# Two-level last product of attention and feed-forward: later first loads, one turn of the PSUM banks, S3's results by way of GpSimd, stores carried into the next product

## The chip, the cores and the metric

The kernel runs on one core of a Trainium2 chip. The metric is the device time of one execution in microseconds (us). Five engines work beside each other, each on its own queue in order: TensorE (PE; its weight loads are listed as PEld), VectorE (DVE), ScalarE (ACT), GpSimd (POOL) and SyncE (SP), which here issues nearly all DMAs. An instruction that waits holds up everything behind it on its own queue.

## The reference, cut to what matters

All arrays are float32; B = 8, H = 12, S = 448, D = 64.

```python
q_n, k_n = rmsnorm(q, g_q), rmsnorm(k, g_k)
scores = (1 / np.sqrt(D)) * np.matmul(q_n, k_n.transpose(0, 1, 3, 2))
attn = softmax(scores)                       # over the last axis
x = np.matmul(attn, v).transpose(0, 2, 1, 3).reshape(B * S, H * D)   # 3584 x 768
h = x @ w_in                                 # 768 x 2048
g = np.maximum(h, 0.0) ** 2
out = g @ w_out                              # 2048 x 768 -> 3584 x 768
```

## The kernel before, in words

The eight batches are worked on in four spans of two. In each span the attention gives x transposed (`xT`, features on partitions, two batches of 448 tokens beside each other), the first product gives g transposed (`gT`), and the second product gives the output transposed, which is turned back and stored. While the second product of a span runs, the attention of the next span is interleaved with it. The last span has no attention beside it, and it is the only one that the change touches.

Both products use Strassen's scheme in its form with seven products of blocks, named A11, S2, S1, S3, A12, A22, S4 by the weights that they use. Sums of the weights are made once at the start and written to DRAM (`w1s`, `w2s`); sums of the right-hand side are made on the chip (`xC` and part of `xT` for the first product; `gC` and part of `gT` for the second, by `combine`, L1021, four subtractions for each f).

`first_product` (L1034) loops over f = 0 to 7. For each f it runs seven groups of three products of 128x128 by 128x448 (each is two rows in the profile). The groups add up in the PSUM tiles `pa`, `pb`, `pc`, `pd`: pa takes A11, then A12; pb S2; pc S1, then S4; pd S3, then A22. VectorE adds the intermediate sums (z, L1075; y, L1078; the results, L1083), ScalarE applies Relu (L1040), GpSimd squares (L1044). The weights of a group (`sw`, 192 KB) are loaded by SyncE through five buffers: before group k the load of group k + 4 is issued (L665, L1066). Counted over all f the groups are u = 0 to 55, N1 = 56.

`bank` (L460) deals out two PSUM banks in turn, one for each call: pb, pc, pd take three of them for each f.

`last_product` (L1144) is the second product of the last span. Its seven products come in the order A11, A12, S2, S1, S3, A22, S4 (o = 0 to 6). Each has three output blocks of 128x448, m = 0, 1, 2. Blocks 0 and 1 are made by a second level of the same scheme, with seven runs of four products of 128x128 by 128x224 (eight rows each): pa (a11), pb (s2), pc (s1), pd (s3), pa (a12), pd (a22), pc (s4). Block 2 is made plainly by `third` (L1227), with eight products by 128x448. The second level needs sums of the weights (`add_weights`, L1173: four GpSimd additions of 128x512) and of the right-hand side (`add_g`, L1185: four VectorE subtractions of 128x896); those of product o + 1 are made during product o. `load_set` (L1168) loads the 1.5 MB of weights of one product with one DMA; there are two sets, `qk` (o even) and `wb` (o odd), so `load_set(o + 2)` follows the end of product o.

A result of the outer scheme has a base, to which the product is added, and a destination. The list `into` (L1217) names them: A11 sets the tile p1s, A12 gives an output from p1s, S2 adds to p1s, S1 gives ys from p1s, S3 has two (an output from ys, and p1s added to), A22 gives an output from p1s, S4 one from ys. Where there is a base, `based` (L1252) lets GpSimd add it to the intermediate sum beforehand (za, zb from z; yb from y; 128x224 each), and `meet` (L1246) lets VectorE add the PSUM tile and write the destination. pd's second run (a22) adds to the tile that `meet(1, 1, ...)` reads, so it has to wait for that.

`send` calls `deliver` (L1137) for an output: VectorE transposes the block by 32x32 into a tile `osb` (L1139; two buffers), and four DMAs store it (L1142), on SyncE's queue unless others are named. Of the last product, S4, the third block comes last and in two halves of 224 columns, with its stores on the queues of SyncE and ScalarE.

At the end of the program (L1367 on) the last product's first two sets are loaded before the first product of the last span starts; add_weights(0) is called in its middle (u = 28), and all four add_g of product 0 after u = 54, ahead of the group S4 of f = 7. The order on each engine is the order of the program text; no planner changes it. In that order, for VectorE around the change of products: L1083 of f = 7 for A22, L1031, L1032, four add_g (L1191), L1083 for S4, then combine(7).

Of the kernel before, what the change touches and what calls it, by code (L numbers as in the profile page):

```python
# [10 lines left out]
F32 = mybir.dt.float32  # L11
# [376 lines left out]
def attention_then_ffn_bounded(  # L388
# [71 lines left out]
    def bank(name, n=None):  # L460

        turn[0] += n is None
        return ps_m.tile([P, S], F32, tag="mn"[turn[0] % 2 if n is None else n], name=name)
# [570 lines left out]
    def first_product(work, span):  # L1034
# [11 lines left out]
        for f in range(HF):  # L1046
# [6 lines left out]
            for at, i in enumerate(order):  # L1053
# [33 lines left out]
                if span and f == HF - 1 and i == S4:  # L1087
                    combine(f)
# [48 lines left out]
    def deliver(work, span, ct, col, t, queues=(nc.sync,), part=slice(0, S // 32)):  # L1137
        osb = work.tile([P, S // 32, 32], F32, tag="osb", name="osb")[:, part]
        nc.vector.transpose(osb.rearrange("p g n -> p (g n)"), ct[:, part.start * 32:part.stop * 32])  # L1139
        for i in range(0, P, 32):  # L1140
            queue = queues[i // 32 % len(queues)]
            queue.dma_start(rows[2 * span + t, :, part, col * P + i:col * P + i + 32], osb[i:i + 32])  # L1142

    def last_product(pool):  # L1144
# [13 lines left out]
        dead = [gT[:, f, 0:S] for f in range(HF)]  # L1158
        used = [0]
# [33 lines left out]
        def small_of(name):  # L1193
            return work.tile([P, HS], F32, tag=name, name=name, bufs=1)
# [4 lines left out]
        ys = dead[0:HC]  # L1199

        def place():
            used[0] += 1
            return dead[HC + used[0] % (HF - HC)]
# [5 lines left out]

        for o, i in enumerate(order):  # L1210
# [12 lines left out]
            def send(m, queues=(nc.sync,)):  # L1223
                if leaves:
                    deliver(work, NSPAN - 1, into[0][1][m], m + at[0], at[1], queues)

            def third():  # L1227
                m = HC - 1
                for part in (slice(0, HS), slice(HS, S)) if end else (slice(0, S),):
                    ps = bank("ps")[:, part]  # L1230
                    for c in range(HF):
                        nc.tensor.matmul(ps, weights_of(o, m, c // HK)[:, c % HK], rhs_of[i][:, c, part],  # L1232
                                         start=c == 0, stop=c == HF - 1)
                    for base, dst in into:
                        if base is None:
                            nc.scalar.copy(dst[m][:, part], ps)
                        else:
                            nc.vector.tensor_tensor(dst[m][:, part], base[m][:, part], ps, add)
                    if end:
                        deliver(work, NSPAN - 1, into[0][1][m], m + at[0], at[1], (nc.sync, nc.scalar),  # L1240
                                slice(part.start // 32, part.stop // 32))
                if not end:
                    add_g(o + 1, 0)
                    send(m)

            def meet(m, t, x, ps):  # L1246

                part = slice(t * HS, (t + 1) * HS)
                for (base, dst), left in zip(into, x):
                    nc.vector.tensor_tensor(dst[m][:, part], left, ps, add)  # L1250

            def based(m, t, x, name):  # L1252
                part = slice(t * HS, (t + 1) * HS)
                all = []
                for n, (base, _) in enumerate(into):
                    if base is None:
                        all.append(x)
                        continue
                    all.append(small_of(f"{name}{n}"))
                    nc.gpsimd.tensor_tensor(all[-1], x, base[m][:, part], add)  # L1260
                return all
# [5 lines left out]
            if not end:  # L1267
                third()
# [7 lines left out]
            nc.vector.tensor_tensor(y, z, pc, add)  # L1276
            add_g(o + 1, 1)
            y22 = based(1, 1, y, "yb")
            pd = ps_o.tile([P, S], F32, tag="t", name="pd")[:, 0:HS]
            run(pd, s3, t3)  # L1280
            meet(1, 1, y22, pd)
            run(pa, a12, b21, False)
            if into[0][0] is None:
                nc.scalar.copy(into[0][1][0][:, 0:HS], pa)
            else:
                meet(0, 0, [base[0][:, 0:HS] for base, _ in into], pa)
# [3 lines left out]
            send(1)  # L1290
            run(pc, s4, b22, False)
            meet(0, 1, z12, pc)
            send(0)
            add_g(o + 1, 3)
            load_set(o + 2)
            add_weights(o + 1)
            if end:
                third()
# [68 lines left out]
    with tc.tile_pool(name="last_product", bufs=2, reuse_waits="tile") as last:  # L1367
        rest = last_product(last)
        load_set, add_weights, add_g = next(rest)
        load_set(0)  # L1370
        load_set(1)
        with tc.tile_pool(name="first_product", bufs=2, reuse_waits="tile") as work:
            for u, _ in enumerate(first_product(work, NSPAN - 1)):
                if u == N1 // 2:
                    add_weights(0)
                if u == N1 - 2:
                    for n in range(4):
                        add_g(0, n)
        with tc.tile_pool(name="second_product", bufs=2, reuse_waits="tile") as work:
            rest.send(work)  # L1380
# [88 lines left out]
```

## Time and profile before

| | us |
|---|---|
| median of 3 runs | 1370.83 (1367.7 to 1371.66) |
| the profiled execution | 1369.9 |
| its span in the trace | 1368.0 |
| first product of the last span, first matmul | 1100.29 |
| last product, first matmul | 1234.17 |
| last product, last group of matmuls starts | 1355.23 |
| TensorE busy | 1337.3, 98% of the span |
| VectorE / GpSimd / ScalarE busy | 876.0 / 624.3 / 431.2 |

The mean granted TensorE clock of the span is 0.993. Times in the trace count from the span's start. In lists of groups, the busy time of a group and the mean of one instruction are followed by the idle time of its engine just before it and by what ended that idle time ("<-DVE gT L1083" is: a VectorE instruction of line 1083 that writes gT). In a table of waits, a line has the total, the number of waits and the longest. Where several rows of a timeline are merged, the row gives its number (x8); a time in brackets is the idle time before it. Each float32 matmul of the program shows as two rows of the list, so a run of four in the last product has eight.

### The profile page before, as it was taken

The numbers are of one execution on the slowest core, as the hardware profiler recorded it, in microseconds if no ns is written. First come the engines' busy times: TensorE is split into PE (matmuls) and PEld (weight loads), VectorE is DVE, ScalarE is ACT, GpSimd is POOL, SyncE is SP. The second block draws the span as 40 slices with busy tenths as digits, with TensorE's granted clock in tenths as the row PEclk, the third lists the DMA queues.
The fourth block names the chain that finished last, engine by engine and source line by source line (L and its number), as shares of the span: only waits on it lengthen the run. The fifth ranks groups of instructions, "written<-read, shape, count | busy, mean of one in ns | idle before, by whom it ended". The sixth has DMA issues, their size and how long they took to land.

```text
span 1368.0 us, 17269 instructions
## 1 busy us (share of the span) xinstructions
PE 1337.3 (98%) x5786; PEld 675.0 (49%) x5786; DVE 876.0 (64%) x1541; ACT 431.2 (32%) x680; POOL 624.3 (46%) x507
## 2 busy tenths in 40 slices
PE   8999999999999999999999999999999989998998
PEld 3333444444444555544444455444444445556877
DVE  6999788599986334478788433458787613335554
ACT  7886565433332111233333011233333101110000
POOL 4767434465573123555664122635656212322553
PEclk9999999999999999999999999999999999999999
DMA  9767998655675423346676433344764453321323
GB/s 243 228 202 203 338 350 312 186 120 118 133 141 126 102 87 86 104 111 135 130 143 130 106 87 88 100 113 109 153 130 107 104 169 87 87 75 46 113 71 86
DMA packets 413814, 190.15 MB, mean 139 GB/s; under 512 B 282388, under 2 KB 408724, under 8 KB 413716
## 3 DMA queue, kind: packets, MB, share of 16 engines
q1 hardware_dynamic: 408020, 180.44, 51.2%
q0 software_dynamic: 4736, 8.40, 2.3%
q8 instruction: 48, 0.79, 0.2%
q14 instruction: 50, 0.41, 0.1%
q10 hardware_dynamic: 960, 0.11, 0.1%
HBM read 155.72 MB, written 33.16 MB: 138 GB/s over the span
## 4 chain that ended last, share of the span: by engine, by line
PE 86%; DVE 6%; ACT 3%; DMA 2%; issue 1%; POOL 1%; SPq 0%; DVEq 0%; ACTq 0%
PE ps L1106 28%; PE pa L1068 10%; PE pd L1068 9%; PE pc L1068 9%; PE sc L785 7%; PE pav L862 7%; PE pb L1068 5%; PE ps L1232 3%; PE pd L1207 2%; ACT gT L797 1%; PE pc L1207 1%; PE pa L1207 1%; DMA sw<-w1s 1%; DVE gT L810 1%; DVE rstd L715 1%
## 5 line engine op out<-in xcount | busy, mean ns | idle before, releaser
L1044 POOL TENSOR_TENSOR gT<-gT 128x448 f32<-128x448 f32 x96 | 94.4, 985 | 294.1 <-ACT gT L1040 294.1
L1106 PE MATMUL ps<-gT,sw 128*128 128x448 f32 x576 | 225.8, 543 | 0.0
L750 POOL TENSOR_TENSOR half<-half,mhalf 128x28 f32<-128x28 f32 x36 | 174.9, 4860 | 73.4 <-DVE half L749 70.1
L1106 PE MATMUL ps<-gC,sw 128*128 128x448 f32 x432 | 170.1, 543 | 0.0
L1106 PEld LDWEIGHTS ps<-gT,sw 128*128 128x128 f32 x576 | 107.5, 190 | 113.9 <-issue 110.3
L1068 PE MATMUL pa<-xT,sw 128*128 128x448 f32 x384 | 157.2, 546 | 5.9 <-DMA sw<-w1s 5.2
L1040 ACT ACTIVATE gT<-gT 128x448 f32<-128x448 f32 x96 | 55.4, 577 | 315.7 <-DVE gT L1083 315.7
L1106 PEld LDWEIGHTS ps<-gC,sw 128*128 128x128 f32 x432 | 80.6, 190 | 86.3 <-issue 83.4
L787 ACT ACTIVATE pr<-sc 128x896 f32<-128x896 f32 x87 | 77.5, 915 | 123.0 <-PE sc L785 123.0
L1068 PEld LDWEIGHTS pa<-xT,sw 128*128 128x128 f32 x384 | 73.5, 192 | 79.1 <-issue 77.2
L785 PE MATMUL sc<-qkT 64*64 64x448 f32 (+1 forms) x1152 | 109.8, 496 | 0.0
L583 POOL TENSOR_TENSOR gC<-gC 128x384 f32<-128x384 f32 x64 | 76.3, 1211 | 62.7 <-DVE gC L579 61.0
L1083 DVE TENSOR_TENSOR gT<-z,pd 128x448 f32<-128x448 f32 x32 | 19.8, 620 | 105.4 <-PE pd L1068 105.4
L830 POOL DMA_DIRECT2D xT<-factors x72 | 38.0, 532 | 91.0 <-DMA factors<-square 53.9
L1068 PE MATMUL pd<-xT,sw 128*128 128x448 f32 x192 | 77.9, 542 | 1.4 <-DVE z L1075 1.4
L1068 PE MATMUL pd<-xC,sw 128*128 128x448 f32 x192 | 77.5, 540 | 1.3 <-DVE gT L1083 1.3
L1068 PE MATMUL pc<-xT,sw 128*128 128x448 f32 x192 | 77.5, 540 | 0.3 <-DMA sw<-w1s 0.3
L1068 PE MATMUL pb<-xC,sw 128*128 128x448 f32 x192 | 77.5, 540 | 0.2 <-DVE gT L1083 0.2
L1068 PE MATMUL pc<-xC,sw 128*128 128x448 f32 x192 | 77.4, 539 | 0.0
L752 POOL TENSOR_TENSOR qk<-qk,half 128x448 f32<-128x448 f32 x72 | 75.5, 1069 | 2.8
L862 PE MATMUL pav<-pr,vt 64*64 64x448 f32 x348 | 72.7, 537 | 0.0
L862 PE MATMUL rest<-pr,vt 64*64 64x448 f32 x348 | 72.7, 537 | 0.0
(217 smaller groups left out, 2175.4 us busy)
## 6 DMA issues: line engine op xcount, KB each, us to landing
sw<-w1s SPq DMA_DIRECT2D x224, 192.0 KB, 2.4
sw<-w2s SPq DMA_DIRECT2D x126, 256.0 KB, 3.4
w1s<-gC SPq DMA_DIRECT2D x8, 1344.0 KB, 6.4
w2s<-gC SPq DMA_DIRECT2D x8, 1344.0 KB, 6.1
out_dram<-osb SPq DMA_DIRECT2D x188, 56.0 KB, 1.8
qk<-in_q_dram SPq DMA_DIRECT2D x144, 56.0 KB, 3.5
qk<-in_k_dram SPq DMA_DIRECT2D x144, 56.0 KB, 2.9
xT<-factors POOLq DMA_DIRECT2D x72, 112.0 KB, 3.3
```

The costliest lines, as they stand in the source:

```text
L583: nc.gpsimd.tensor_tensor(*[blocks_of(n)[:, place_of(n, i)] for i in (dst, x, y)], op)
L750: nc.gpsimd.tensor_tensor(half, half, mhalf, ALU.pow)
L752: nc.gpsimd.tensor_tensor(qkn[:, s], raw[:, s], half[:, s * NG:(s + 1) * NG].rearrange("p g -> p g ()").to_broadcast([P, NG, 32]), ALU.mult)
L785: nc.tensor.matmul(sc[part, h, 0:n], qkT[rows, 0, 1, keys], qkT[rows, 0, 0, of], start=True, stop=True)
L787: nc.scalar.activation(pr, sc[:, :, 0:n], AF.Exp)
L862: nc.tensor.matmul(into, vs[i][rows, h, c, :], probs[i, c][rows, h, :], start=(c == 0), stop=(c == NF), skip_group_check=True)
L1040: nc.scalar.activation(g, src, AF.Relu)
L1044: nc.gpsimd.tensor_tensor(g, g, g, ALU.mult)
L1068: nc.tensor.matmul(ps, stream[n + at][:, c], rhs[:, c], start=first and c == 0, stop=c == HC - 1, skip_group_check=not first)
L1106: nc.tensor.matmul(ps, stream[n][:, c % 4], rhs_of[i][:, c], start=c == 0, stop=c == HF - 1)
L1207: nc.tensor.matmul(ps, lhs[:, c], rhs[:, c], start=first and c == 0, stop=c == HK - 1, skip_group_check=not first)
L1232: nc.tensor.matmul(ps, weights_of(o, m, c // HK)[:, c % HK], rhs_of[i][:, c, part], start=c == 0, stop=c == HF - 1)
```

## The change

Five things are done, all in the last span:

1. Its first loads: load_set(0) and load_set(1) are called after u = 14 and u = 21 of the first product rather than before it.
2. One turn of its banks: `turn[0] += 1` ahead of the last product, so its tiles take the other one of the two banks. Of the add_g of product 0, two stay after u = 54, two are called after u = 55, ahead of combine(7).
3. Two results of S3: VectorE writes the product's blocks 0 and 1 once, into tiles `block`, with no base (pa's half by a copy on ScalarE), and GpSimd adds each of them to its two bases (`settle`, four additions of 128x448).
4. Sums of weights: add_weights(o + 1) is called behind the run of s3 rather than at the end of product o.
5. Stores: blocks 1 and 0 of a product are not delivered at its end but in the next product, behind its third block (`late`), ahead of that product's own block 2. In S4 the third block is second in order as in all others, blocks 1 and 0 come last, and block 0 is stored in two halves. The blocks' places (`dead`) are no longer used in turn.

In the changed kernel's order on VectorE, A22 and S4 have, behind the addition of the third block (and add_g, in A22), three transposes in a row: block 1 and block 0 of the product before, then their own block 2; then zi.

```diff
-                if span and f == HF - 1 and i == S4:
+                if span and f == HF - 1 and i == S4 and span + 1 < NSPAN:
                     combine(f)
...
-        dead = [gT[:, f, 0:S] for f in range(HF)]
-        used = [0]
+        dead = [gT[:, f, 0:S] for f in range(NFC)]
+        used, late = [0], []
...
+        blocks = [work.tile([P, S], F32, tag="block", name="block") for _ in range(2)]
...
-            return dead[HC + used[0] % (HF - HC)]
+            return dead[HC - 1 + used[0]]
...
+        turn[0] += 1
         for o, i in enumerate(order):
...
-            def send(m, queues=(nc.sync,)):
-                if leaves:
-                    deliver(work, NSPAN - 1, into[0][1][m], m + at[0], at[1], queues)
+            def send(m, part=slice(0, S // 32)):
+                deliver(work, NSPAN - 1, into[0][1][m], m + at[0], at[1],
+                        (nc.sync, nc.scalar) if end else (nc.sync,), part)
+
+            both = len(into) > 1
...
-            def meet(m, t, x, ps):
+            def meet(m, t, left, ps):
 
                 part = slice(t * HS, (t + 1) * HS)
-                for (base, dst), left in zip(into, x):
-                    nc.vector.tensor_tensor(dst[m][:, part], left, ps, add)
+                dst = blocks[m] if both else into[0][1][m]
+                nc.vector.tensor_tensor(dst[:, part], left, ps, add)
 
             def based(m, t, x, name):
-                part = slice(t * HS, (t + 1) * HS)
-                all = []
-                for n, (base, _) in enumerate(into):
...
+                base = into[0][0]
+                if both or base is None:
+                    return x
+                y = small_of(name)
+                nc.gpsimd.tensor_tensor(y, x, base[m][:, t * HS:(t + 1) * HS], add)
+                return y
+
+            def settle(m):
+                for base, dst in into if both else ():
+                    nc.gpsimd.tensor_tensor(dst[m], base[m], blocks[m], add)
...
             nc.scalar.copy(p1, pa)
-            if not end:
-                third()
+            third()
+            add_g(o + 1, 0)
+            for args in late:
+                deliver(*args)
+            late[:] = []
+            if leaves:
+                send(HC - 1)
             pb = ps_o.tile([P, S], F32, tag="o", name="pb")[:, 0:HS]
             run(pb, s2, t2)
...
             run(pd, s3, t3)
+            add_weights(o + 1)
             meet(1, 1, y22, pd)
             run(pa, a12, b21, False)
...
             meet(1, 0, z21, pd)
-            send(1)
+            settle(1)
+            if end:
+                send(1)
+                send(0, slice(0, HS // 32))
             run(pc, s4, b22, False)
             meet(0, 1, z12, pc)
-            send(0)
+            settle(0)
+            if end:
+                send(0, slice(HS // 32, S // 32))
+            elif leaves:
+                for m in (1, 0):
+                    late.append((work, NSPAN - 1, into[0][1][m], m + at[0], at[1]))
             add_g(o + 1, 3)
             load_set(o + 2)
-            add_weights(o + 1)
-            if end:
-                third()
...
-        load_set(0)
-        load_set(1)
         with tc.tile_pool(name="first_product", bufs=2, reuse_waits="tile") as work:
             for u, _ in enumerate(first_product(work, NSPAN - 1)):
+                if u in (14, 21):
+                    load_set(u // 7 - 2)
                 if u == N1 // 2:
                     add_weights(0)
                 if u == N1 - 2:
-                    for n in range(4):
-                        add_g(0, n)
+                    add_g(0, 0)
+                    add_g(0, 1)
+                if u == N1 - 1:
+                    add_g(0, 2)
+                    add_g(0, 3)
+                    combine(HF - 1)
```

## The prediction

> **What bounds the kernel now.** I read the shares of busy time first, then the chain that ended last, then who waited for whom in the last 270 us (the diff touches nothing earlier), then the timeline around each wait found, and last the granted clock in short windows.
>
> ```profile
> PE 1337.3 (98%) x5786; PEld 675.0 (49%) x5786; DVE 876.0 (64%) x1541; ACT 431.2 (32%) x680; POOL 624.3 (46%) x507
> PE 86%; DVE 6%; ACT 3%; DMA 2%; issue 1%; POOL 1%; SPq 0%; DVEq 0%; ACTq 0%
> ```
>
> TensorE bounds the kernel; the change leaves its matmuls as they are (the last product of S4 only takes its third block whole and sooner), so only TensorE's waits and the tail behind its last matmul can move. The table of waits, 1100 us to the end, has three long ones on TensorE:
>
> ```profile
> PE pa L1068 <- DMA sw<-w1s: 5.2, 1, 5.2
> ...
> PE ps L1232 <- DVE gT L1083: 3.5, 1, 3.5
> ...
> PE pd L1207 <- DVE p L1250: 2.1, 1, 2.1
> ```
>
> Each costs more than its length. Windows of 3.413 us over the last product (columns: stretch, its length, busy us of PE, PEld, DVE, ACT, POOL, granted clock, DMA share, GB/s):
>
> ```profile
> 1235.25:1238.67 3.42, 0.60 (x4) 0.25 (x2) 3.32 (x5) 0.00 (x0) 0.00 (x0) 0.97 0.00 0
> 1238.67:1242.08 3.41, 2.74 (x4) 1.51 (x5) 1.76 (x3) 0.81 (x2) 2.11 (x2) 0.50 0.00 0
> 1242.08:1245.49 3.41, 3.41 (x6) 1.44 (x5) 3.34 (x3) 0.00 (x0) 3.33 (x4) 0.53 0.00 0
> 1245.49:1248.91 3.42, 3.42 (x12) 1.93 (x11) 2.98 (x3) 0.26 (x1) 1.50 (x1) 1.00 0.02 5
> ...
> 1320.58:1324.00 3.42, 1.31 (x7) 0.93 (x6) 1.61 (x5) 0.00 (x0) 3.41 (x5) 0.97 0.04 6
> 1324.00:1327.41 3.41, 3.41 (x11) 3.12 (x10) 2.19 (x4) 0.00 (x0) 3.34 (x3) 0.53 0.00 0
> ```
>
> A window in which TensorE is busy 0.60 or 1.31 us is followed by half speed until a full window has passed. Windows with 2.05 and 2.12 us busy (around 190 and 145 us; waits of 1.36 and 1.29 us) kept the whole clock. So a wait over about 2 us inside one window also costs 1.7 to 3.4 us of clock, and one of 1.3 us does not.
>
> [...] combine's subtractions take 0.62 us alone and 1.57 to 1.70 us beside add_weights. [...] the small stores here land 1.9 us after issue (median, 1.7 to 3.8). [...] In the trace a w1s block issued right behind the two w2s sets took 9.7 us to land, against a median of 2.4.
>
> **The change, part by part** (times on before's clock).
>
> *First loads later.* load_set(0) and load_set(1) leave SyncE's queue ahead of the w1s blocks. Now TensorE's fifth group of the first product starts at 1114.71 and the next at 1119.17. Unhindered, at the pitch of 2.255 us a group, that next one would start at 1107.06 + 2 x 2.255 = 1111.57. Gain 7.6 us. The sets (1.5 MB each, 6.4 and 8.2 us to land) now go out at groups 14 and 21; the block issued 2.25 us behind one is needed 4 x 2.255 = 9.0 us after its own issue and should land after some 8.2 - 2.25 + 1 = 7 us. That slack of 2 us hides it; without it the price is a wait like the old one, twice. add_weights(0) follows set 0 by 14 groups, 31 us, and is hidden.
>
> *One turn of the banks; add_g split.* The third block of A11 gets the bank that pd used, read at 1232.74, instead of pc's, read at 1239.28. It starts at 1235.68 rather than 1239.34 and takes 6.02 us rather than 9.06: 6.7 us. What is late next is VectorE. Its queue from 1233.73 to meet: add_g 1.9 and 1.0 us, L1083 0.5, add_g 1.0 and 2.0 (beside add_weights), combine 5.4 (three at 1.6, one at 0.55), add_g 1.05, zi and yi 0.65, add_g 1.0, meet 0.4, in all 14.9: 1248.6. pd's second run is due at 1241.70 + 4 x 1.51 = 1247.75, and waits for meet. Loss 1.0, with contention to the end 1.6; I take 1.2, below the length that costs clock (bounds 0 and 2.4). Net gain 5.5.
>
> *S3's two results.* Now six GpSimd additions stand ahead of VectorE's meet; pd's second run starts at 1323.22, due 1320.95, and 16 matmuls then take 4.82 us for 3.03. After: no addition ahead of meet, one meet for two. Gain 2.27 + 1.79 = 4.1. The added part is a copy of pa on ScalarE (0.34, idle there) and four GpSimd additions of 128x448, 1.0 to 1.3 us each by the rows L1044 (985 ns) and L1179 (1.3 to 1.5 for 512): about 5 us at the start of A22. Their first reader is 7.7 us in, so I take nothing. add_weights(5) moves ahead of them and beside add_g: meet then ends about when due (bounds 0 and 0.5).
>
> *add_weights sooner.* On GpSimd it stands behind yb in both kernels except in S3: nothing.
>
> *Stores carried over (late).* This is the part with a price. Transposes of blocks 1 and 0 move from the end of a product to just ahead of zi in the next, behind its third block. In S2 two, of 0.57 us each, stand there: zi 1.1 later, yi not (it waited 1.05 for pc), yb and meet 0.9 later with slack 0.5: loss 0.4 (0 to 0.8). In A22 and S4 there are three transposes in a row, and osb has two buffers: the third waits until the first one's four stores have landed, and zi is queued behind it on VectorE; za, zb, yb, meet and TensorE's pd wait for zi. A22 now, from the timeline:
>
> ```profile
> 1335.76 0.62 DVE L1238 TENSOR_TENSOR gT<-p,ps 128x448 f32<-128x448 f32 x1 [5.31 <-PE ps L1232]
> 1336.30 1.08 DVE L1191 TENSOR_TENSOR xC<-gT 128x896 f32<-128x896 f32 x1
> ...
> 1337.30 0.64 DVE L1139 STREAM_TRANSPOSE osb<-gT 128x448 f32<-128x448 f32 x1
> 1337.87 0.35 DVE L1272 TENSOR_TENSOR zi<-p1i,pb 128x224 f32<-128x224 f32 x1
> ...
> 1341.07 0.39 DVE L1250 TENSOR_TENSOR gT<-yb,pd 128x224 f32<-128x224 f32 x1 [0.55 <-POOL yb L1260]
> ...
> 1341.62 1.68 PE L1207 MATMUL pd<-xT,wb 128*128 128x224 f32 x8
> ```
>
> meet ends at 1341.46, 0.16 ahead of pd. How long a buffer is taken shows in the chain at the kernel's end, where a transpose ended at 1355.00:
>
> ```profile
> 1355.02 0.32 SPq L1142
> ...
> 1355.38 0.48 SPq L1142
> ...
> 1355.90 0.49 SPq L1142
> ...
> 1356.44 0.49 SPq L1142
> ```
>
> The fourth store issues 1.44 us after the transpose and lands 1.9 later, or 1.9 after the issue's end: 3.35 to 3.8, plus 0.2 in which VectorE steps through four semaphores (1362.18 to 1362.38 in the same chain). I take 3.7. So the third transpose of A22 starts at 1337.94 + 3.7 = 1341.6 instead of 1337.3: 4.3 late, less the slack: 4.1 us of TensorE wait (3.5 to 5.8, with 3.6 for a slow landing as the last one in the chain). That empties over half of one window: clock 1.7 to 3.4, I take 2.3. Together 6.4.
>
> S4, from its third block's end E: addition to E+0.74, first transpose to E+1.4, third from E+5.1, zi to E+6.05, three GpSimd additions at 0.62 to E+8.0, meet to E+8.4; pd is due at E+6.05. Loss 2.4 (1.9 to 4.1). The clock may halve the 1.5 us run behind: 0.7 (0 to 1.5).
>
> *The end.* Now the last transpose starts 1.1 us after TensorE's last matmul. After, it needs the buffer of block 1, which is transposed after pd's second run ends at P: transposed by P+1.3, stores on two queues (two issues each, to P+1.9), landing 2.2, semaphores 0.3: P+4.4. TensorE ends at P+1.51, so now-like would be P+2.6. Loss 1.8 (0.5 to 3.5). A slow clock on the last run hides in it.
>
> Sum: -7.6 - 5.5 - 4.1 + 0.4 + 6.4 + 3.1 + 1.8 = -5.5 us. The profiled execution took 1369.9 (span 1368.0 and 1.9 around it), so 1364.4; the median of three runs is 0.93 above it: 1365.3.
>
> **Rivals.** *No buffer wait* (stores land before the third transpose, or zi is not late by it): the losses of late and end shrink to 0.4, giving -16.8, 1354. Against it, the order on VectorE puts zi behind, and no store here landed under 1.7 us. *Slow landings, slower than before*: mechanism and place are the third transpose's wait in A22 and S4 and the last one at the end. With landing time L in place of 1.9, the loss grows by 3 (L - 1.9), so the gain is gone at L = 3.7 and 0.3% is lost at L = 5.1, or at 4.2 with both clock losses full (+1.9) and VectorE's A11 queue at its worst (+1.2). For it: the chain ends in a landing of 3.57, just where stores are dense; against: the median of 1.9 over 52. At L = 4.4, about 1375. *Sets still collide with w1s blocks*: two waits of 2 us plus 1.8 of clock eat the first gain: +2, 1373. Against: each set now goes alone, with 9 us of lead. *The turn frees nothing*, because meet is then as late as the bank was: the 5.5 falls to 2, 1369; it is inside the main case's bounds.
>
> **How the numbers follow.** 0.3% is 4.1 us, about what a measurement of this kernel can tell from no change. Bounds of the terms run from -10.8 (1360) to +3.6 (1374.4), ends that need all terms at once. Chances: main case 0.74 (own range 1361 to 1369; about 0.58 of it below 1366.7), no buffer wait 0.08, slow landings 0.09, colliding sets 0.09. Faster 0.58 + 0.08 = 0.66; same 0.16 + 0.09 (the sets) + 0.01 = 0.26; slower the rest of slow landings, 0.08. Range 1360 to 1371.5, which leaves out most of the rivals.
>
> **What would show it.** After: no wait of TensorE on sw<-w1s; the first ps of the last product without a wait and pd of A11 waiting about 1 us on VectorE; no wait in S3; two new waits of VectorE's transposes on out_dram of 2 to 3 us, followed by TensorE's pd waiting about 4.1 and 2.4 us with windows at half clock; a wait of 2 us at the last transpose. Wrong if the transposes find their buffers free, or if w1s blocks still come late.

## The result, and the profile after

| | before | after |
|---|---|---|
| median of 12 runs each, same chip (us) | 1371.63 (1367.7 to 1373.91) | 1369.02 (1366.66 to 1370.06) |
| ratio, 95% interval | | 0.9976 (0.9966 to 0.9985) |
| span of the profiled execution | 1368.0 | 1367.1 |
| from the first matmul of the last span to the end | 267.7 | 265.7 |

The change is faster by 0.24%, 2.1 to 4.7 us by the interval. The forecast was 5.5 us (0.40%) and 1365.3. It had the direction and the places of the waits, and it made the losses too small: the median lies at the upper end of the range that the prediction gave its main case (1361 to 1369), and the gain just under the 0.3% that it called faster, with that bound inside the interval. On TensorE the last span divides as follows (us; each stretch runs from the first matmul of one product to that of the next, the last one to the span's end). The parts of the program before this span are the same in all kernels here but differ by up to 2.9 us from one profiled execution to another, so stretches are compared, not spans.

| | first product | A11 | A12 | S2 | S1 | S3 | A22 | S4 and end |
|---|---|---|---|---|---|---|---|---|
| before | 133.88 | 23.31 | 16.68 | 16.60 | 16.61 | 20.67 | 16.60 | 23.36 |
| after | 126.28 | 18.58 | 16.67 | 17.13 | 16.61 | 16.61 | 23.53 | 30.29 |
| difference | -7.60 | -4.73 | 0 | +0.53 | 0 | -4.06 | +6.93 | +6.93 |

A product without any wait takes 16.6. Three gains make 16.4 us. Three losses make 14.4; all of them lie where part 5 works, which carries stores over and also changes S4's order.

The busy time and the shares of the chain, from the page of after. TensorE has nearly the share of before, and its busy time fell by only 1.8 us:

```profile
PE 1335.5 (98%) x5770; PEld 671.9 (49%) x5770; DVE 875.6 (64%) x1535; ACT 431.8 (32%) x681; POOL 627.2 (46%) x505
...
PE 87%; DVE 7%; ACT 2%; issue 1%; DMA 1%; POOL 1%; SPq 0%; DVEq 0%; ACTq 0%; POOLq 0%
```

The table of waits of after from 1085 us to the end (total, number, longest). The waits of TensorE on `sw<-w1s` (5.2), for a bank (3.5) and in S3 (2.1) are no longer in it. In their place VectorE waits three times for a store buffer. Two of these come back as waits of pd, in A22 and S4 (second line). The last line has the waits of pd in A11 (1.70) and S2 (0.26):

```profile
DVE osb L1139 <- DMA out_dram<-osb: 9.6, 3, 3.4
...
PE pd L1208 <- DVE gT L1247: 6.7, 2, 4.4
...
PE pd L1208 <- DVE p L1247: 2.0, 2, 1.7
```

The timeline of TensorE in after where the first wait was. Groups now follow each other every 2.255 us; the one that began at 1119.17 begins at 1112.68, 11.28 after the first matmul of the span, exactly where the prediction's pitch puts it:

```profile
1108.17 2.42 PE L1068 MATMUL pd<-xT,sw 128*128 128x448 f32 x6
1110.42 2.42 PE L1068 MATMUL pa<-xT,sw 128*128 128x448 f32 x6
1112.68 2.42 PE L1068 MATMUL pd<-xC,sw 128*128 128x448 f32 x6
```

VectorE's timeline of after around the third block of A22 (start, busy time, work; in brackets the idle time before it and what ended it):

```profile
1321.54 1.08 DVE L1191 TENSOR_TENSOR xC<-gT 128x896 f32<-128x896 f32 x1
1322.55 1.16 DVE L1139 STREAM_TRANSPOSE osb<-gT 128x448 f32<-128x448 f32 x2
1327.14 0.65 DVE L1139 STREAM_TRANSPOSE osb<-gT 128x448 f32<-128x448 f32 x1 [3.43 <-DMA out_dram<-osb]
1327.71 0.35 DVE L1275 TENSOR_TENSOR zi<-p1i,pb 128x224 f32<-128x224 f32 x1
...
1330.97 0.39 DVE L1247 TENSOR_TENSOR gT<-yb,pd 128x224 f32<-128x224 f32 x1 [1.16 <-POOL yb L1254]
```

The third transpose starts 3.9 us after the end of the first (1323.20), which is how long the buffer was taken. zi stands behind it, GpSimd's yb behind zi, meet (L1247) behind yb. TensorE's timeline of after then shows the same wait in A22 and again in S4, and each time slow matmuls behind it (eight rows of a run take 1.68 at full clock):

```profile
1331.41 3.36 PE L1208 MATMUL pd<-xT,wb 128*128 128x224 f32 x8 [4.39 <-DVE gT L1247]
1334.56 2.41 PE L1208 MATMUL pc<-gC,qkT 128*128 128x224 f32 x8
...
1352.83 3.12 PE L1208 MATMUL pd<-xC,qk 128*128 128x224 f32 x8 [2.28 <-DVE gT L1247]
1355.74 2.07 PE L1208 MATMUL pc<-gT,qkT 128*128 128x224 f32 x8
```

The granted clock of after changes at 1329.21, 1336.04, 1353.10, 1356.52 and 1359.93, times that are 3.413 us apart or a multiple of it. The windows of after around A22, cut at these times (columns as in the prediction), show that the wait falls into two of them. Each leaves TensorE busy for 1.22 us and is followed by half clock. The third is wholly busy, and the whole clock comes back behind it:

```profile
1325.80:1329.21 3.41, 1.22 (x7) 0.87 (x5) 1.97 (x4) 0.00 (x0) 1.01 (x2) 1.00 0.65 100
1329.21:1332.63 3.42, 1.22 (x3) 1.15 (x4) 2.26 (x4) 0.00 (x0) 3.34 (x4) 0.50 0.34 55
1332.63:1336.04 3.41, 3.41 (x10) 3.07 (x10) 0.86 (x2) 0.00 (x0) 3.41 (x3) 0.50 0.00 0
1336.04:1339.45 3.41, 3.41 (x17) 2.84 (x15) 1.39 (x2) 0.35 (x1) 0.64 (x1) 1.00 0.00 0
```

The shorter wait of S4 falls into one window, and one runs at half clock:

```profile
1349.69:1353.10 3.41, 1.13 (x6) 0.78 (x5) 1.77 (x5) 0.00 (x0) 1.89 (x3) 1.00 0.72 108
1353.10:1356.52 3.42, 3.42 (x11) 3.09 (x11) 0.50 (x2) 0.00 (x0) 0.00 (x0) 0.50 0.03 7
```

The chain of after at its end (start, us, what). An earlier landing, with stores on SyncE's queue alone, took 1.89 us; pd's slow run is on it, and then the landing of block 1's stores, 3.50 us, ahead of the last transpose:

```profile
1347.45 1.89 DMA out_dram<-osb
...
1352.83 3.13 PE pd L1208 x8
...
1355.99 0.40 DVE gT L1247
...
1357.44 3.50 DMA out_dram<-osb
...
1361.16 0.41 DVE osb L1139
```

The 3.50 us count from the start of the store's issue, and the issue is a large part of them. SyncE's timeline of after has it at 1.46 us, while the issues ahead of the earlier landing took 0.3 to 0.5 each:

```profile
1357.44 1.46 SPq L1142 DMA_DIRECT2D out_dram<-osb  x1
```

### The profile page after: what moved, and what is told of

The parts are those of the page before. It is cut to its first block, busy times and chain, and to the rows that moved or that the text cites. A ratio compares the mean times of both kernels' runs of the same rounds, so it can differ in the third digit from the quotient of the medians.

```text
span 1367.1 us, 17241 instructions
## 1 busy us (share of the span) xinstructions
PE 1335.5 (98%) x5770; PEld 671.9 (49%) x5770; DVE 875.6 (64%) x1535; ACT 431.8 (32%) x681; POOL 627.2 (46%) x505
## 4 chain that ended last, share of the span: by engine, by line
PE 87%; DVE 7%; ACT 2%; issue 1%; DMA 1%; POOL 1%; SPq 0%; DVEq 0%; ACTq 0%; POOLq 0%
PE ps L1106 28%; PE pd L1068 10%; PE pa L1068 10%; PE pc L1068 10%; PE sc L785 7%; PE pav L862 7%; PE pb L1068 5%; PE ps L1235 3%; PE pd L1208 1%; ACT gT L797 1%; PE pc L1208 1%; PE pa L1208 1%; DVE gT L810 1%; PE sc L793 1%; DVE rstd L715 1%
```

## The experiments

The theory: three parts gain what the first product, A11 and S3 show, and the stores carried over give most of it back, because zi stands behind a transpose that waits for a store buffer. The rivals: the gains are smaller by themselves, or the losses come from something else that the change does (the new order at the end of S4, the additions on GpSimd). The table has the result of each run, the ratio to before with its interval, and those stretches that differ from 16.6. The last column is the whole last span. The experiments were run on three chips, each beside before (medians 1370.24, 1370.48 and 1371.27), so ratios are compared rather than medians. The stretches come from one profiled execution of each kernel. It can lie some us from the median: that of combine_later took 1363.76 us, the least of its 20 runs, which go up to 1371.29.

| | median | ratio | first product | A11 | S2 | S3 | A22 | S4 and end | last span |
|---|---|---|---|---|---|---|---|---|---|
| before | | 1 | 133.88 | 23.31 | | 20.67 | | 23.36 | 267.7 |
| after | 1369.02 | 0.9976 (0.9966 to 0.9985) | 126.28 | 18.58 | 17.13 | | 23.53 | 30.29 | 265.7 |
| loads_only | 1360.94 | 0.9925 (0.9905 to 0.9946) | 126.28 | 22.05 | | 18.98 | | 23.7 | 257.5 |
| turn_only | 1365.41 | 0.9962 (0.9949 to 0.9976) | 134.54 | 18.62 | | 18.97 | | 23.6 | 262.2 |
| settle_only | 1368.82 | 0.9989 (0.9980 to 0.9997) | 134.29 | 23.29 | | | 17.71 | 23.66 | 265.5 |
| no_late | 1359.73 | 0.9920 (0.9897 to 0.9943) | 126.28 | 18.61 | | 16.75 | | 27.28 | 255.5 |
| osb3 | 1359.97 | 0.9923 (0.9901 to 0.9945) | 126.28 | 18.56 | 17.13 | | 17.72 | 27.04 | 256.6 |
| late_behind | 1363.54 | 0.9948 (0.9931 to 0.9965) | 126.28 | 18.63 | | | | 31.64 | 259.6 |
| end_whole | 1366.94 | 0.9978 (0.9969 to 0.9987) | 126.28 | 18.58 | 17.13 | | 22.93 | 28.74 | 263.6 |
| osb3_whole | 1359.70 | 0.9927 (0.9900 to 0.9954) | 126.28 | 18.63 | 17.13 | | 17.71 | 26.53 | 256.2 |
| old_end | 1363.14 | 0.9950 (0.9932 to 0.9968) | 126.28 | 18.62 | 17.13 | | 23.69 | 24.55 | 260.2 |
| combine_later | 1366.77 | 0.9974 (0.9964 to 0.9983) | 126.28 | | 17.13 | | 22.90 | 29.42 | 262.3 |
| best2 | 1357.11 | 0.9913 (0.9889 to 0.9937) | 126.27 | | | | | 28.3 | 254.4 |
| best3 | 1355.30 | 0.9886 (0.9853 to 0.9919) | 126.28 | | | | | 25.27 | 251.2 |

### One part alone

**loads_only**: the kernel before with the later loads.

```diff
-        load_set(0)
-        load_set(1)
...
             for u, _ in enumerate(first_product(work, NSPAN - 1)):
+                if u in (14, 21):
+                    load_set(u // 7 - 2)
```

> The kernel before with part 1 alone (both first loads moved to groups 14 and 21 of the first product). Theory of added terms (each part is worth what its own stretch showed): no wait of TensorE on a w1s block, 7.6 us less than before, ratio 0.9945. Rival (the loads only move their collision, or the gain is paid back in the last product): under 4 us, ratio above 0.997.

The wait is gone and the first product has exactly the 7.60 us. The last span gained 10.2 us, because A11 and S3 became shorter too (1.3 and 1.7), though nothing of them was changed and their waits kept their length (3.5 and 2.1). The whole program after the first product moved against the windows of the clock. S3's wait lay inside one window in before (first two lines). In loads_only it is divided between two, and the clock stays whole (last two):

```profile
1320.40:1323.81 3.41, 1.30 (x7) 0.95 (x6) 1.42 (x5) 0.00 (x0) 3.41 (x5) 1.00 0.09 14
1323.81:1327.22 3.41, 3.41 (x11) 3.09 (x10) 2.28 (x4) 0.00 (x0) 3.33 (x3) 0.50 0.00 0
...
1309.81:1313.22 3.41, 1.94 (x11) 1.59 (x9) 0.98 (x2) 0.00 (x0) 3.41 (x5) 1.00 0.33 51
1313.22:1316.63 3.41, 2.77 (x15) 2.77 (x16) 3.12 (x7) 0.00 (x0) 3.33 (x3) 1.00 0.00 0
```

Behind A11's wait one window runs at half clock where before had two (the third block's matmuls behind it take 7.97 us, where before's took 9.22). So the clock's price of a wait was not a constant of the wait: with a wait of 2.1 us S3 took 20.67 us in before and 18.98 here, by where in the windows it fell.

**turn_only**: the kernel before with the turn of the banks and the split of add_g.

```diff
-                if span and f == HF - 1 and i == S4:
+                if span and f == HF - 1 and i == S4 and span + 1 < NSPAN:
...
+        turn[0] += 1
...
-                    for n in range(4):
-                        add_g(0, n)
+                    add_g(0, 0)
+                    add_g(0, 1)
+                if u == N1 - 1:
+                    add_g(0, 2)
+                    add_g(0, 3)
+                    combine(HF - 1)
```

> The kernel before with part 2 alone (the other bank; two add_g and combine behind the addition of S4). Added terms: the wait of 3.5 us and its half clock go, pd of A11 waits 1.5 to 1.9 us on VectorE instead: 4.7 to 4.9 us less, ratio 0.9965. Rival (the A11 queue of VectorE gives it back): 0 to 2 us, ratio 0.9985 or more.

As expected: A11 takes 18.62. S3 is again 1.7 us shorter without being changed, with the same wait of 2.1 and the whole clock (pd's run behind the wait takes 1.78 us). What is late next is what the prediction named, VectorE's queue; meet stands at its end. In after the same is seen in VectorE's timeline: one of the four subtractions of combine, beside GpSimd's additions, takes 1.68 us where it took 0.62 alone, and meet comes at 1242.69.

```profile
1226.70 0.62 DVE L1032 TENSOR_TENSOR gT<-gT 128x448 f32<-128x448 f32 x1
...
1238.29 1.68 DVE L1032 TENSOR_TENSOR gT<-gT 128x448 f32<-128x448 f32 x1
...
1242.69 0.38 DVE L1247 TENSOR_TENSOR p<-yi,pd 128x224 f32<-128x224 f32 x1
```

**settle_only**: the kernel before with S3's two results by way of blocks and GpSimd (the parts of the diff with `blocks`, `both` and `settle`), stores as before.

```diff
             meet(1, 0, z21, pd)
+            settle(1)
             send(1)
...
             meet(0, 1, z12, pc)
+            settle(0)
             send(0)
```

> The kernel before with part 3 alone (S3's blocks written once, settled by GpSimd); the stores stay at the product's end, so two transposes now wait for GpSimd there. Added terms: no wait in S3, 4.1 us less, ratio 0.9970. Rival (GpSimd's four additions come too late for the transposes and hold up VectorE and so A22): 0 to 2 us.

S3's 4.06 us came, but A22 lost 1.1 of them, and the first product and the end are 0.7 us longer together. The last span is 2.2 us shorter and the ratio 0.9989: the expected 4.1 us and 0.9970 were missed, and the rival's size (0 to 2 us) is the nearer one. Its path was half right. The timeline of GpSimd in settle_only shows why: add_weights(5) (L1179) is not yet moved ahead, so it stands behind the four additions of settle and comes late, beside VectorE's next add_g:

```profile
1329.01 1.13 POOL L1265 TENSOR_TENSOR p<-p,block 128x448 f32<-128x448 f32 x1
1330.10 2.14 POOL L1179 TENSOR_TENSOR xT<-wb 128x512 f32<-128x512 f32 x1
...
1334.77 1.28 POOL L1179 TENSOR_TENSOR qkT<-wb,xT 128x512 f32<-128x512 f32 x1
```

VectorE's timeline of settle_only: that add_g takes 2.20 us where it took 1.08, and a transpose waits for GpSimd's sum:

```profile
1326.85 0.65 DVE L1139 STREAM_TRANSPOSE osb<-gT 128x448 f32<-128x448 f32 x1 [1.25 <-POOL gT L1265]
...
1334.80 2.20 DVE L1191 TENSOR_TENSOR xC<-gT 128x896 f32<-128x896 f32 x1
```

zi, yb and meet follow later, and pd waits 0.84. So "add_weights sooner: nothing" holds only beside before's S3. Beside the new S3 it seems to keep about 1 us of the third gain: in no_late below, which also stores at the product's end but has add_weights moved ahead, A22 takes 16.7. No run changes add_weights alone.

### The stores carried over

**no_late**: after, with blocks 1 and 0 sent at the end of their own product.

```diff
             settle(1)
+            if leaves:
+                send(1)
             if end:
-                send(1)
                 send(0, slice(0, HS // 32))
...
             elif leaves:
-                for m in (1, 0):
-                    late.append((work, NSPAN - 1, into[0][1][m], m + at[0], at[1]))
+                send(0)
```

> The changed kernel with the stores of blocks 1 and 0 back at their product's end (part 5 undone, S4's order of blocks kept). Theory: the waits of 4.5 and 2.3 us in A22 and S4 with their half clock (6.9 and 3.8) and S2's 0.5 go, the last transpose keeps its wait: some 11 us less than the changed kernel, 13 less than before, ratio to before 0.990. Rival (these losses come from S4's order of blocks, or from the settled results, not from the carried stores): within 3 us of the changed kernel, ratio 0.996 or more.

The waits of S2, A22 and S4 are gone, and the last span is 10.2 us shorter than after's. Two transposes wait 1.3 us each for GpSimd's sums in S3, but no matmul of TensorE waits for them. S4 and the end still take 27.28, which is 3.9 us more than in before: the last transpose waits 4.1 for a buffer. This part of the loss belongs to S4's order of blocks and not to the stores carried over.

**osb3**: after, with three store buffers in the last span.

```diff
-        osb = work.tile([P, S // 32, 32], F32, tag="osb", name="osb")[:, part]
+        osb = work.tile([P, S // 32, 32], F32, tag="osb", name="osb", bufs=3 if span + 1 == NSPAN else 2)[:, part]
```

> The changed kernel with three buffers for osb in the last product instead of two. Theory (the carried stores cost through the wait for a buffer, with zi queued behind it): no wait of a transpose on out_dram in A22 and S4 nor at the end; A22 keeps about 1 us of wait for the two extra transposes; 5.9 + 4.2 + 3 = some 13 us less than the changed kernel, ratio to before 0.989. Rival (what costs is that transposes and stores stand ahead of zi at all): within 3 us of the changed kernel, ratio 0.9955 or more.

A22 falls from 23.53 to 17.72 and S4's wait of 2.28 is gone: the buffer was the cause, as `late` itself is unchanged here. A wait of pd of 0.84 is left in A22, about the 1 us expected for two more transposes ahead of zi. The end missed its expectation. The last transpose starts right behind the last matmuls, but 9.15 us pass from its end to the span's end, against 5.5 in after (1361.57 to 1367.1). The table of waits of SyncE's queue in osb3 has a new line, a store that waits 3.0 us for an earlier store:

```profile
SPq L1142 <- DMA out_dram<-osb: 3.0, 1, 3.0
```

**late_behind**: after, with all stores of a product moved behind `meet(1, 1, ...)`.

```diff
-            for args in late:
-                deliver(*args)
-            late[:] = []
-            if leaves:
-                send(HC - 1)
...
             meet(1, 1, y22, pd)
+            for args in late:
+                deliver(*args)
+            late[:] = []
+            if leaves:
+                send(HC - 1)
```

> The changed kernel with the stores carried over, and the third block's, moved behind meet of block 1 instead of ahead of zi, still two buffers. Theory (zi stands behind the buffer wait on VectorE): the waits of pd in A22 and S4 go, A22 takes 16.6 instead of 23.5, S2 too loses nothing; in S4 the buffer wait moves to the tail, where S4 and the end take 26 to 28 us instead of 30.3; together 10 to 11 us less than the changed kernel, near 1358.5. Rival (in S4 the transposes behind meet pile up and end as late as in the changed kernel): 7.5 us less, near 1361.5.

S2 and A22 are back at 16.6 with two buffers: what cost TensorE its time is that zi stood behind the waiting transpose. But the rival was right for S4. The waits moved behind the additions and into its tail: VectorE's line in the table of waits of late_behind has five, one in A22 (4.34) and four in S4. S4 with the end takes 1.35 us more than in after:

```profile
DVE osb L1139 <- DMA out_dram<-osb: 14.0, 5, 4.4
```

### The end of S4

**end_whole**: after, with block 0 of S4 stored whole instead of in two halves (one transpose fewer).

```diff
             if end:
                 send(1)
-                send(0, slice(0, HS // 32))
...
-                send(0, slice(HS // 32, S // 32))
+                send(0)
```

> The changed kernel with S4's block 0 stored whole at the end rather than in two halves, so that the last transpose finds the other buffer, free for long. Theory (the last wait, 2.9 us, is for block 1's stores, which land 3.5 us after issue because the half block's stores run beside them): no wait, last transpose 2.6 to 3.2 us sooner, itself 0.2 longer: 2 to 3 us less than the changed kernel, ratio to before 0.9955. Rival (stores at the end land late whatever is beside them, so that the bigger last store pays it back): within 1 us of the changed kernel.

The last transpose waits for nothing now and starts at 1357.75 instead of 1361.16, but the end comes only 1.6 us sooner after the last matmul (7.7 us for 9.3). In this trace the end gains less than the theory's 2 to 3 us and more than the rival's 1. By the ratios (0.9978 and 0.9976) the kernel cannot be told from after, and the theory's 0.9955 is out.

**osb3_whole**: both edits together, to see whether fewer stores shorten the tail where no buffer is waited for.

```diff
-name="osb")[:, part]
+name="osb", bufs=3 if span + 1 == NSPAN else 2)[:, part]
...
-                send(0, slice(0, HS // 32))
...
-                send(0, slice(HS // 32, S // 32))
+                send(0)
```

> osb3 (three store buffers) with block 0 of S4 stored whole instead of in two halves, so eight stores instead of twelve stand at the end (block 1 and block 0). Theory (number of stores in flight sets the tail): from TensorE's last matmul to the end about 7.7 us instead of 10.3, near 1357.4. Rival (the tail is the time of any store behind others on its queue): no change from osb3's 1360.

The rival: no change from osb3. What holds the tail can be read from this trace. From the end of the last transpose (1349.25) to the end 8.65 us pass. SyncE's queue in osb3_whole issues its last two stores, which belong to that transpose, only at 1352.36, and the wait ahead of them is one for a store:

```profile
SPq L1142 <- DVE osb L1139: 11.3, 2, 9.4
SPq L1142 <- DMA out_dram<-osb: 3.7, 1, 3.7
```

The trace does not show which store. The times fit one of block 1, whose stores on ScalarE's queue were issued from 1347.77 and 1348.18 on. The slowest landing of this stretch, by the group of stores of osb3_whole, took 4.1 us:

```profile
DMA to landing us min/median/max: 1.7/2.7/4.1
```

As an estimate, 1348.18 + 4.1 = 1352.3, where SyncE goes on. The wait for a buffer, once removed, is taken over by a wait of SyncE's queue for an earlier store (3.7 us), and by this estimate that one too ends when a store of block 1 lands.

**old_end**: after, with S4 ordered at its end as before (blocks 1 and 0 stored whole as they come, the third block last and in two halves). The lines that make the halves and their stores are left out here.

```diff
...
-            third()
+            if not end:
+                third()
...
             load_set(o + 2)
+            if end:
+                third()
```

> The changed kernel with the last product (S4) ordered at its end as before: blocks 1 and 0 stored whole as they are made, the third block last of TensorE's work, in two halves of 224 columns with their stores behind each; the two transposes carried over from A22 stay ahead of zi in S4. Theory (the order of S4 costs the end, because the changed order makes three blocks' stores fall within some 3 us): S4 and the end take 23.4 to 24.2 us as before, against 30.3 in the changed kernel, so about 6.3 us less, near 1362.7; A22 still loses its 6.9. Rival (stores drain as slowly whichever block comes last, and only the buffer wait in S4 is saved): 26.5 to 27.5, about 3 us less, near 1366.

S4 and the end fall by 5.7 to 24.55, so the rival of a slow drain in any order is out. A22 keeps its loss (7.1 here). The third block's matmuls give the stores of blocks 1 and 0 6.22 us to land, and S4's pd doesn't wait: ahead of its zi stand only two transposes. Of S4's loss of 6.9 us, the new order without the carried stores costs 3.9 (no_late), and the carried stores without the new order cost 1.2 here; the rest comes only where both are. In the table of waits of old_end one wait of each kind is left where after had three and two:

```profile
PE pd L1208 <- DVE gT L1250: 4.4, 1, 4.4
DVE osb L1139 <- DMA out_dram<-osb: 3.4, 1, 3.4
```

### The wait of A11, and the versions that beat both

**combine_later**: after, with `combine(HF - 1)` moved behind `meet(1, 1, ...)` of A11.

```diff
                     add_g(0, 3)
-                    combine(HF - 1)
...
             meet(1, 1, y22, pd)
+            if o == 0:
+                combine(HF - 1)
```

> The changed kernel with combine(7) called behind meet(1, 1) of A11 instead of ahead of the last product. Theory (pd of A11 waits for VectorE's queue, 6.5 us of it combine beside add_weights): that wait of 1.7 us goes, 1.9 us less than the changed kernel, ratio to before 0.996, and the first wait of pd on VectorE is gone from the trace. Rival (the contention only moves: combine then holds up A12): the wait appears in A12, no change.

A11 takes 16.61 and its wait is gone, so the wait was VectorE's queue and not the bank. The last span gained 3.4 in the profile, of which A11 is 2.0; the rest comes from A22 (22.90 for 23.53) and S4 (29.42 for 30.29), where the clock halved for a shorter time or not at all (mean granted clock of the profiled execution 0.996 for 0.992). But the profiled execution was the fastest of its runs, and by the two ratios (0.9974 and 0.9976) the kernels can't be told apart; the expected 0.996 was missed.

**best2**: combine later, four store buffers, and the stores behind `meet(1, 1, ...)` in all products but S4.

```diff
+name="osb", bufs=4 if span + 1 == NSPAN else 2)[:, part]
...
+            if end:
+                stores()
             pb = ps_o.tile([P, S], F32, tag="o", name="pb")[:, 0:HS]
...
             meet(1, 1, y22, pd)
+            if o == 0:
+                combine(HF - 1)
+            if not end:
+                stores()
```

Here `stores` is what stood ahead of zi: the transposes and DMAs in `late`, then the third block's.

> All parts of the change, with four buffers for osb, combine(7) behind meet(1, 1) of A11, and the carried stores behind meet(1, 1) in every product but S4, where they stay ahead of zi. Theory of added terms, against the changed kernel: A11 -1.9, S2 -0.5, A22 -6.9, S4 -4.2, end -3: 16 to 17 us less, ratio to before 0.986 to 0.987, no wait of TensorE over 0.5 us in the last span. Rival (a new wait takes the place of each): no less than 1357 us.

**best3**: best2 with S4's end as before.

```diff
-            third()
+            if not end:
+                third()
...
             load_set(o + 2)
+            if end:
+                third()
```

The lines on halves and stores are left out as above.

> best2 (four store buffers, stores behind meet of block 1, combine later) with the end of S4 as before: third block last, in two halves. Theory: S4 and the end take 23.4 us instead of 28.3, all else as in best2, so about 5 us less than best2's 1357.1: near 1352, a ratio of about 0.986. Rival (the end is bound by the drain of the stores in any order): within 1.5 us of best2.

In both, TensorE waits for nothing in the last span: A11 to A22 take 16.6 each. best2 still missed its ratio of 0.986 to 0.987, because S4 and the end take 28.3; its rival (a new wait takes the place of each, no less than 1357 us) was right. best3 has the lowest median of all, 0.9886 (0.9853 to 0.9919) of before. Its step over best2 is 3.2 us in the profile, less than the 5 expected, and by the intervals of the two ratios they can't be told apart. 8.45 us pass from TensorE's end to the span's end, against 6.55 before. Its last transpose waits 0.8 us for landings (first line). SyncE's queue waits for earlier stores too (second line): block 1, whose transpose ended at 1338.08, has its first store there only at 1339.93.

```profile
DVE osb L1139 <- DMA out_dram<-osb: 0.8, 1, 0.8
...
SPq L1142 <- DMA out_dram<-osb: 6.6, 3, 6.1
```

## Why the prediction was right, and where it was off

**First loads**: forecast -7.6, measured -7.60, also alone. The new loads hinder no later block: no wait on `sw<-w1s` is left.

**Turn of the banks, add_g**: forecast -5.5, measured -4.73 and alone -4.69 (18.62 against 23.31). The gain of 6.7 was right for before's profile: 23.31 - 16.6. The loss on VectorE was taken at 1.2 and is 2.0: pd starts 1.86 us late, its run takes 0.1 more, and the clock stays whole (1.00 from 1242 to 1246). It lies inside the bounds given (0 to 2.4). The mis-sized term is combine: the prediction had three of its subtractions at 1.6 and one at 0.55, and VectorE's timeline under turn_only has that one at 1.68 too. combine_later shows that VectorE's queue is the cause.

**S3**: forecast -4.1, measured -4.06. The copy on ScalarE and GpSimd's four additions cost TensorE nothing in after. That the size agrees so well is in part luck: 1.7 us of the gain are clock that before's profiled execution paid and loads_only and turn_only did not, with the same wait.

**Stores in S2**: forecast +0.4, measured +0.53.

**Stores in A22**: forecast 4.1 of wait and 2.3 of clock; measured 4.39, and the two runs behind it took 2.4 more (3.36 - 1.68 and, to the next run's start, 2.25 - 1.51). Both windows of the wait, with TensorE busy 1.22 us in each, were followed by half clock, as the prediction read it from before's windows with 0.60 and 1.31. (Its windows were cut 0.2 us beside the clock's own, 0.60 us busy for 0.78; that changes none of its bounds.) The size again depends on where the wait falls: with waits of 4.37 to 4.39, A22 took 22.90 to 23.69 us in combine_later, end_whole, after and old_end.

**Stores in S4**: forecast 2.4 of wait and 0.7 of clock; the wait was 2.28. The mis-sized term is the clock: pd's run took 3.12 for 1.68, so 1.4, and pc's 0.4 more. The prediction took half of "0 to 1.5". A middle value was all that could be said ahead here, since the price came out at 1.8 us in after and at nothing elsewhere: in combine_later S4's pd waits 2.35 and the clock stays whole; the window that holds most of the wait keeps 1.50 us of work, where after's kept 1.13:

```profile
1344.73:1348.14 3.41, 1.50 (x8) 1.15 (x7) 1.31 (x4) 0.00 (x0) 1.88 (x3) 1.00 0.77 117
1348.14:1351.56 3.42, 2.98 (x16) 2.95 (x16) 1.81 (x5) 0.00 (x0) 0.00 (x0) 1.00 0.11 20
```

**The end**: forecast +1.8, measured +2.8 (9.3 from TensorE's end against 6.55). The mechanism, a last transpose that needs block 1's buffer, is on the chain. With P the end of pd's second run (1355.96), the prediction had the stores issued by P + 1.9 and landed 2.2 later; they were issued by P + 2.9 (1357.44 + 1.46) and landed 2.0 later (1360.94). So the landing behind the issue was sized rightly, and the mis-sized term is the issue, two stores on each of two queues in 0.6 us; it took 1.8. From the start of its issue to its landing a store took 1.89 us in mid-product and 3.50 here.

Together the forecast sum of -5.5 and the measured -2.0 differ by 3.5 us: 0.8 from A11, 0.1 from S2, 0.5 from A22, and 2.0 from S4 and the end (4.9 forecast, 6.93 measured). The medians of 12 differ by 2.6. All terms were worked out on one profiled execution of before, and since that one's waits paid the clock that they happened to meet, agreement to a few tenths is more than the method can promise. The rival "no buffer wait" is what osb3 and no_late build: 1360 rather than the 1354 worked out, because the end stays long in both. "Slow landings" was half right: in after they are slow at the end, and the waits in A22 and S4 have nearly the forecast length. (By that rival's own sum its bound of 4.2 us is 4.1.) "The turn frees nothing" and "sets still collide" are out by turn_only and loads_only.

**What stays open**: why a store at the end takes 3.5 us from issue to landing where one in mid-product takes 1.9, and why its issue takes 1.46. Two queues at once, the density, or both could do it; no run here separates them. Against density alone speaks that in after eight stores in a row on SyncE's queue, from 1345.7 to 1349.4, landed within 1.7 to 2.0; against two queues alone that in osb3 one on that queue, issued at 1344.96 behind others on both, took 3.26. Which earlier store SyncE's queue waits for in osb3_whole, and what ties the two, was not shown; that it is one of block 1 is an estimate from the times. Before's tail of 6.55 us after a third block in halves was not reached in old_end (7.74) with the same order of work but blocks 1 and 0 on two queues; that difference was not followed.

## What to carry to other kernels

When a step is carried into later work, look at what it may wait for and at what then stands behind it on its engine: a transpose that waited 4.34 us for a store buffer in A22 cost TensorE nothing behind `meet(1, 1, ...)` (late_behind, 16.6), and the stores carried over cost 6.9 us there ahead of an addition that TensorE needs (after). Count buffers against steps in a row (three transposes, two buffers). Price a wait with the clock as a range: here a wait of 2.1 to 2.4 us cost no clock or nearly a whole window at half speed, by where it fell. At the end of this kernel it paid to leave matmuls behind the stores, not the reverse; taking away one wait there (2.93 us in after, for a buffer) showed the next (3.7 us in osb3_whole, on SyncE's queue), which also ends with the landing of a store.

## What was not expected of the hardware

- Stores at the end land later after the start of their issue: 3.50 us (after, of which 1.46 is the issue) and 4.1 at most (osb3_whole), against 1.9 in mid-product.
- The price of the clock was not fixed by the length of a wait: with waits of the same length (3.5 and 2.1), A11 and S3 took 23.31 and 20.67 us in before, and 22.05 and 18.98 in loads_only.
- In windows of 3.413 us, cut at the times at which the clock changed, half clock came behind those that left TensorE least to do. In the traces of before and after, from 20 us after the start to the last matmul, the windows at full clock with 0.71, 0.79 and 1.30 us busy (before, from 1108.77, 1235.06 and 1320.40) and with 1.22 and 1.13 (after, from 1325.80 and 1349.69) were followed by half clock. No other was; the least busy of the others had 2.12 in before (from 20.02) and 1.72 in after (from 1240.46). In combine_later one with 1.50 (from 1344.73) kept the whole clock. These figures are no fixed bound: at the start of after, a window with 1.46 us (from 18.49) was followed by half clock too.
- On the way back, windows at half clock with 0.89 and 2.55 us busy (before, from 1112.18 and 1238.48) and with 1.22 (after, from 1329.21) were followed by another at half clock; the three in before and two in after that TensorE filled (3.41 or 3.42) were followed by the whole clock.
- By length of wait: A11's 1.70 us in after left 1.72 us busy in its window and cost no clock. Those of S3 and S4 came out both ways: 2.1 us with half clock in before and without in loads_only, 2.28 us with it in after and 2.35 without in combine_later. That of A22 had half clock behind it at 4.39 us in after, and at 4.37 in old_end (pd's run took 3.36 us in both).
